# The attention's rows go to DRAM through GpSimd's DMA queue instead of SyncE's

## The chip, the cores and the metric

One Trainium2 chip (trn2), one of its cores. The time is device microseconds (us) of one execution of the program; the profile is one further execution of the same program, taken by the hardware profiler. The engines are named as the profile names them: PE (TensorE, matrix products), PEld (its weight loads), DVE (VectorE), ACT (ScalarE), POOL (GpSimd) and SP (SyncE, which computes nothing and starts DMAs). POOLq and SPq are the instruction queues of the last two, where their DMA starts stand.

## The reference

Block-causal attention for 8 batches of 8 heads, 576 tokens of 64 numbers, and then a mixture of 8 experts over the 4608 tokens of 512 numbers, of which each token takes the best one:

```python
scores = q @ k.T / sqrt(64)                  # per batch and head, 576 x 576
scores = where(row // 64 >= col // 64, scores, -1e9)
attn = exp(scores - max); attn /= attn.sum(-1) + 1e-09
x = (attn @ v)  ->  4608 rows (batch, token) of 512 (head, d)
logits = x @ w_gate                          # 8 experts
e = argmax(logits); g = softmax(logits)[e]; eom = sigmoid(x @ w_output_gate)
out[row] = g * eom[e] * (relu(x @ w1[e]) @ w2[e])
```

## The kernel before

**Stages.** The attention runs until about 420 us, the experts from there to the end at 825 us; the two overlap a little, since the first expert's work begins between the last pairs of heads. Rows of the attention's result pass from the one to the other through a DRAM buffer, `x_d` (4608 x 512 f32), from which the experts gather their tokens by index. A table in DRAM, `tab_d`, holds for each expert which rows are its own.

**One batch.** A batch is two units of four heads (16 units, u0 to u15), a unit is two pairs of heads (32 pairs). For each unit the function `Load` fetches k and q (`nat`, L91, 576 KB each), splits each into a high half (the cast of L96, on DVE) and a low half (the subtraction of L97, on POOL), transposes both by DMA (`tr`, L102) and copies two halves crosswise (`sw`, L107 and L108). For each pair, `load_v` loads the values of v (`va` L317, `vb` L319, `v8` L322), `softmax` makes scores on PE (`ps_s`, L335 to L338), their row maxima on DVE (`nmx`, L372, L393, L404) and from these the bias (`nbs`, L343, L406) of the exponentials on ACT (L355); `flip` transposes the probabilities on PE (L423) and copies them out (`pT`, L429); `values` multiplies by v (L438, L452) into `xT` (L453, L454).

**The end of a batch** is `finish_batch`. For each of five row tiles (64 rows, and four times 128) `rows(t)` transposes on PE (L469), normalizes on DVE into `xn` (L472) and writes `xn` to `x_d` (L476). `xn` has two buffers, so the third tile's L472 can only run when the first tile's write has landed, the fourth when the second's has, and so on. Between these rows stands the choice of the expert on DVE (L498 to L563), ending in the slots `sli` (L556) and the weights `idg` (L570), one small product on POOL (`z`, L565), and five scatters on POOL into `tab_d` (L574). After the last batch POOL reads the table (`ids`, L738) and gathers rows (`xg`, L749), which are cut and transposed (`xr`, `xt`) for PE (L889).

**What sets the order.** PE's order is written out by hand: generators (`softmax` of the next pair, `flip` and `values` of the present one, `finish_batch` of the batch before, `load_heads` two units ahead) are stepped in turns. The order of the other engines, and of the DMA starts on SP and POOL, is set when the program is built, by a scheduler that estimates when each instruction could start; each engine then executes its list strictly in that order. Each start of a DMA is an instruction on the engine that starts it; it waits there for its data and its buffer, and all behind it wait too.

```python
            x.split(0, nc.vector.tensor_copy, nc.gpsimd)     # L96 cast on DVE, L97 subtraction on POOL
        tr = sb.tile([P, MAXR, P], F16, name=f"tr{1 - i}")
        nc.sync.dma_start_transpose(tr, ...)                 # L102, on SP
        va = sb.tile([P, 4, D], F32, name="va", bufs=3)
        nc.sync.dma_start(va, v[b, hA, 0:512]...)            # L317, on SP
```

Of the kernel before, what the change touches and what calls it, by code (L numbers as in the profile page):

```python
# [26 lines left out]
def block_attention_top1_moe(  # L27
# [11 lines left out]
    nc = tc.nc  # L39
    B, H, S, D = q.shape  # L40
# [4 lines left out]
    Q0 = [0, 64, 192, 320, 448]  # L45
# [31 lines left out]
    x_d = dram.tile([NTOK, DM], F32, name="x_d")  # L77
# [380 lines left out]
    def finish_batch(b, sums, xT):  # L458
# [5 lines left out]
        def rows(t):  # L464

            r = ROWS[t]
            pm = ps_t.tile([P, 512], F32, name="ps_t")
            for g in range(NP):
                nc.tensor.transpose(pm[0:r, P * g:P * g + P], xT[:, g, Q0[t]:Q0[t] + r], ident)  # L469
            xn = sb.tile([P, DM], F32, name="xn")  # L470
            with tc.high_priority(offset=5):
                nc.vector.tensor_tensor(  # L472
                    xn[0:r].rearrange("p (h d) -> p h d", d=D), pm[0:r].rearrange("p (h d) -> p h d", d=D),
                    rec[0:r, t].unsqueeze(2).broadcast_to([r, H, D]), ALU.mult,
                )
            nc.sync.dma_start(x_d[b * S + Q0[t]:b * S + Q0[t] + r, :], xn[0:r])  # L476

        yield

# [1 line left out]
        for c0, c1 in ((0, 448), (448, 576)):  # L481
# [7 lines left out]
            yield  # L489
        yield  # L490
        rows(0)
        yield
        lh = small.tile([P, NT, H, 16], F32, name="lh", bufs=1)
# [38 lines left out]
        for t in range(1, NT):  # L532
            rows(t)
            yield
# [36 lines left out]
        for t in range(NT):  # L571
            r = ROWS[t]
# [379 lines left out]
    for p in range(B * NP):  # L952
        b, hp = divmod(p, NP)
# [161 lines left out]
```

## Time and profile before

| | |
|---|---|
| time, median of 3 runs | 823.86 us (822.45 to 830.36) |
| profiled execution, its own time | 826.82 us |
| its span from first to last instruction | 825.1 us |
| granted TensorE clock, mean | 0.982 |
| busy: PE, DVE, ACT, POOL | 764.0, 547.1, 517.5, 252.6 us |
| moved by hardware queues (SP) | 127.76 MB |
| moved by the software queue (POOL) | 19.29 MB |

The profiled execution's time is its span and 1.7 us around it, and lies 2.96 us above the median. Busy times say how much of the span an engine had an instruction in hand. An engine's idle time is put down to the event that came last before it went on ("releaser").

### The profile page before, as it was taken

The page shows a single profiled execution, that of the slowest core. Times are in us where ns is not written, and L with a number is a line of the kernel's source. Part 1 is how long each engine was busy: PE and PEld are TensorE (multiplying, and loading weights), DVE is VectorE, ACT ScalarE, POOL GpSimd, SP SyncE. Part 2 cuts the span into 40 slices and gives each one's busy share as a digit, 9 for nine tenths or more (in the row PEclk, how much of TensorE's full clock was granted, in tenths as well). Part 3 has the DMA queues.
Part 4 walks back from the last instruction along what each step waited for, and adds up shares of the span by engine and source line. Part 5 has one row for each costly group of instructions (what it writes and reads, how often), then busy time and mean ns, then how long its engine had stood idle before and what let it go on. Part 6 is the DMA issues. An engine that isn't in the chain of part 4 may idle for free. (4 is left out here: it accounts for less than half of the span.)

```text
span 825.1 us, 17693 instructions
## 1 busy us (share of the span) xinstructions
PE 764.0 (93%) x6466; PEld 512.7 (62%) x6466; DVE 547.1 (66%) x1200; ACT 517.5 (63%) x1207; POOL 252.6 (31%) x219
## 2 busy tenths in 40 slices
PE   4899988898989889778999999999999999999994
PEld 3566656565656656555686666676657666676652
DVE  5787858677676767858572866786566656786530
ACT  5788776777758667567513855765556555775530
POOL 4322312424122242447245432233212333200001
PEclk9999999999999999889999999999999999999998
DMA  8998997989898797996029899793789958721601
GB/s 153 168 185 174 192 176 148 176 150 184 173 205 151 155 183 157 191 226 177 28 83 270 152 369 257 220 275 99 249 264 280 274 188 281 179 50 48 230 27 41
DMA packets 255887, 148.25 MB, mean 180 GB/s; under 512 B 224561, under 2 KB 224625, under 8 KB 255793
## 3 DMA queue, kind: packets, MB, share of 16 engines
q1 hardware_dynamic: 247520, 127.76, 69.4%
q0 software_dynamic: 8272, 19.29, 7.6%
q8 instruction: 53, 0.87, 0.5%
q14 instruction: 42, 0.34, 0.1%
HBM read 122.23 MB, written 19.73 MB: 172 GB/s over the span
## 5 line engine op out<-in xcount | busy, mean ns | idle before, releaser
L889 PEld LDWEIGHTS <-w1b 128*128 128x128 f16 (+1 forms) x2112 | 182.6, 98 | 25.2 <-ACT ys L919 2.0
L355 ACT ACTIVATE pt<-ps_s,nbs 128x448 f32<-128x448 f32 (+1 forms) x314 | 164.4, 535 | 41.8 <-DVE nbs L343 17.9
L889 PE MATMUL ps_s<-xt,w1b 128*128 128x256 f16 (+3 forms) x1824 | 182.1, 261 | 1.8 <-DMA xt<-xr 1.5
L916 PE MATMUL ps_t<-w2b,hh 128*128 128x512 f16 x608 | 181.0, 379 | 0.0
L778 DVE TENSOR_TENSOR w2b<-w2f,w2b 128x1024 bf16<-128x1024 f32 x76 | 88.0, 1219 | 113.4 <-ACT w2b L777 113.4
L423 PE MATMUL ps_t<-ident,pt 128*128 128x128 f32 x800 | 124.5, 283 | 8.2 <-DVE xn L472 3.9
L429 ACT COPY pT<-ps_t 128x512 f32<-128x512 f32 (+3 forms) x222 | 96.5, 463 | 56.4 <-PE ps_t L423 55.6
L97 POOL TENSOR_TENSOR sp<-nat,sp 128x1152 f16<-128x1152 f32 x30 | 71.2, 2374 | 152.8 <-DVE nbs L343 91.7
L916 PE MATMUL ps_t<-w2b,hl 128*128 128x512 f16 x304 | 115.2, 379 | 0.0
L919 ACT ACTIVATE ys<-ps_t,ids 128x512 f32<-128x512 f32 x38 | 26.1, 687 | 136.1 <-PE ps_t L916 112.1
L335 PE MATMUL ps_s<-tr,tr 128*128 128x448 f16 (+1 forms) x378 | 98.8, 284 | 11.4 <-ACT pt L355 10.9
L920 POOL DMA_INDIRECT out_dram<-ys,ids x38 | 44.9, 1181 | 185.0 <-ACT ys L919 130.2
L916 PEld LDWEIGHTS <-hh 128*128 128x128 f16 x608 | 59.3, 98 | 66.8 <-issue 0.2
L423 PEld LDWEIGHTS ps_t<-ident,pt 128*128 128x128 f32 x800 | 87.3, 143 | 15.6 <-DVE xn L472 4.2
L336 PE MATMUL ps_s<-sw,tr 128*128 128x448 f16 (+1 forms) x378 | 91.4, 283 | 1.8 <-DMA sw<-tr 1.3
L438 PE MATMUL ps_a<-pT,va 128*64 128x512 f32 (+3 forms) x256 | 85.5, 457 | 6.8 <-DMA va<-in_v_dram 5.7
L778 DVE TENSOR_TENSOR w1b<-w1f,w1b 128x1024 bf16<-128x1024 f32 x76 | 88.1, 1218 | 0.5 <-ACT w1b L777 0.2
L393 DVE TENSOR_REDUCE nmx<-ps_s 128x2 f32<-128x896 f32 (+1 forms) x63 | 60.2, 955 | 41.7 <-PE ps_s L338 41.1
L438 PE MATMUL ps_a<-pT,vb 128*64 128x512 f32 (+3 forms) x256 | 85.6, 458 | 2.0 <-DMA vb<-in_v_dram 2.0
L777 ACT CAST w1b<-w1f 128x1024 f16<-128x1024 f32 x76 | 74.1, 1045 | 1.2 <-DMA w1f<-in_moe_w_dram 1.2
L777 ACT CAST w2b<-w2f 128x1024 f16<-128x1024 f32 x76 | 73.6, 1042 | 0.0
L355 ACT ACTIVATION_READ_ACCUMULATOR pt<-ps_s,nbs 128x1 f32 x314 | 65.2, 208 | 0.0
(203 smaller groups left out, 1080.2 us busy)
## 6 DMA issues: line engine op xcount, KB each, us to landing
w1f<-in_moe_w_dram SPq DMA_DIRECT2D x76, 512.0 KB
w2f<-in_moe_w_dram SPq DMA_DIRECT2D x76, 512.0 KB
nat<-in_k_dram SPq DMA_DIRECT2D x15, 576.0 KB
nat<-in_q_dram SPq DMA_DIRECT2D x15, 576.0 KB
sw<-tr SPq DMA_DIRECT2D x30, 288.0 KB
x_d<-xn SPq DMA_DIRECT2D x32, 256.0 KB
va<-in_v_dram SPq DMA_DIRECT2D x32, 128.0 KB
vb<-in_v_dram SPq DMA_DIRECT2D x64, 64.0 KB
```

Source lines behind the costliest of these rows:

```text
L97: last_lo[0] = lo.tensor_tensor(sp[:, :, 1, :], self.nats[i], sp[:, :, 0, :], ALU.subtract)
L335: nc.tensor.matmul(ps_ap, qq, k1[ab][:, c0:c1], start=True, stop=False)
L336: nc.tensor.matmul(ps_ap, qq, k2[ab][:, c0:c1], start=False, stop=last)
L355: last_exp[0] = nc.scalar.activation(to, ap, AF.Exp, bias=nbs[0:r, t, ab:ab + 1], scale=SCALE, accum_out=sums[0:r, t, hA + ab:hA + ab + 1],)
L393: nc.vector.tensor_reduce(nmx[:, t, :], pX[:, :, 0:n], AX.X, ALU.max, negate=True)
L423: nc.tensor.transpose(ps[:, i], probs[t][:, col:col + P], ident)
L429: copies[next(nth)](pT[:, r:r + m, Q0[t]:Q0[t] + rows], ps[:, i:i + m, 0:rows])
L438: nc.tensor.matmul(pa[64 * a:64 * a + 64, P * j:512], (va, vb)[a][:, j, :], pT[:, 1 + 2 * j + a, 64 + P * j:576], start=(j == 0), stop=False,)
L777: nc.scalar.copy(hi, src)
L778: eng.tensor_tensor(lo, src, hi, ALU.subtract)
L889: nc.tensor.matmul(ph[:, f4].rearrange("p (h n) -> p h n", n=P), wv[:, cc, f, :], xv[:, cc], start=(k == 0), stop=(k == 3 * KD - 1))
L916: nc.tensor.matmul(py, hv[:, f, h], wv[:, f, :], start=(k == 0), stop=(k == 3 * KF - 1))
```

## The change

All 40 writes of `xn` to `x_d` (8 batches of one write of 128 KB and four of 256 KB) are started by GpSimd instead of SyncE, and so go through the software queue. Nothing else is written differently:

```diff
                     rec[0:r, t].unsqueeze(2).broadcast_to([r, H, D]), ALU.mult,
                 )
-            nc.sync.dma_start(x_d[b * S + Q0[t]:b * S + Q0[t] + r, :], xn[0:r])
+            nc.gpsimd.dma_start(x_d[b * S + Q0[t]:b * S + Q0[t] + r, :], xn[0:r])
```

Since the order of all engines but PE is made anew at each build, the one line moves instructions elsewhere too. The writes leave SP's list and come into POOL's; PE's list is almost as it was; DVE's, ACT's and SP's lists are shuffled from the second batch's rows on.

On SP, the place around the sixth batch's writes and u15's transposes, before (`v_4959` is a pair's `v8`, the two numbered `tr` are those of u15):

```order
190 L476 DMA x_d<-xn 128x512
191 L317 DMA va<-in_v_dram 128x4x64
192 L319 DMA vb<-in_v_dram 64x4x64 x2
193 L322 DMA v_4959<-in_v_dram 128x1x64
194 L476 DMA x_d<-xn 128x512
195 L102 DMA_TRANSPOSE tr_5010<-sp 128x18x128
196 L476 DMA x_d<-xn 128x512
197 L102 DMA_TRANSPOSE tr_5039<-sp 128x18x128
198 L476 DMA x_d<-xn 128x512
199 L107 DMA sw<-tr_5010 64x2304
200 L108 DMA sw<-tr_5010 64x2304
201 L317 DMA va<-in_v_dram 128x4x64
```

And the same place now:

```order
170 L317 DMA va<-in_v_dram 128x4x64
171 L319 DMA vb<-in_v_dram 64x4x64 x2
172 L322 DMA v_4959<-in_v_dram 128x1x64
173 L317 DMA va<-in_v_dram 128x4x64
174 L319 DMA vb<-in_v_dram 64x4x64 x2
175 L322 DMA v_5170<-in_v_dram 128x1x64
176 L102 DMA_TRANSPOSE tr_5010<-sp 128x18x128
177 L102 DMA_TRANSPOSE tr_5039<-sp 128x18x128
178 L107 DMA sw<-tr_5010 64x2304
179 L108 DMA sw<-tr_5010 64x2304
```

The writes are gone, and the `va`, `vb` and `v8` of the pair that stood behind the transposes and the copies now stand ahead of them. The same happens at the transposes of two units before: of u11 (`va` and one `vb` move ahead) and of u13 (`va` and both `vb`).

On POOL, one batch (the first) between two groups of splits. Before:

```order
29 L97 TENSOR_TENSOR sp<-nat,sp 128x18x64 x4
30 L494 MEMSET lh 64x128
31 L565 TENSOR_TENSOR z<-L,oh 128x40
32 L574 DMA tab_d<-idg,sli 37120x2 x5
33 L97 TENSOR_TENSOR sp<-nat,sp 128x18x64 x4
```

And now:

```order
29 L97 TENSOR_TENSOR sp<-nat,sp 128x18x64 x4
30 L476 DMA x_d<-xn 64x512
31 L476 DMA x_d<-xn 128x512
32 L494 MEMSET lh 64x128
33 L476 DMA x_d<-xn 128x512
34 L565 TENSOR_TENSOR z<-L,oh 128x40
35 L476 DMA x_d<-xn 128x512 x2
36 L574 DMA tab_d<-idg,sli 37120x2 x5
37 L97 TENSOR_TENSOR sp<-nat,sp 128x18x64 x4
```

All five writes of a batch stand ahead of the five scatters, and so ahead of the split behind these. In the last batch one write stands between the second and the third scatter. In the sixth batch one of the splits of u15 stands between the first two writes.

On DVE, the cast of u10's k (`sp<-nat`), at the pair of heads that it goes with at about 215 us, before:

```order
380 L393 TENSOR_REDUCE nmx<-ps_s 128x2
381 L343 TENSOR_SCALAR nbs<-nmx 128x1 x2
382 L393 TENSOR_REDUCE nmx<-ps_s 128x2
383 L96 CAST sp<-nat 128x18x64
384 L343 TENSOR_SCALAR nbs<-nmx 128x1 x2
```

And now:

```order
377 L372 TENSOR_REDUCE nmx<-ps_s 128x2
378 L96 CAST sp<-nat 128x18x64
379 L343 TENSOR_SCALAR nbs<-nmx 128x1 x2
380 L372 TENSOR_REDUCE nmx<-ps_s 128x2
381 L429 COPY pT<-ps_t 128x3x128
382 L343 TENSOR_SCALAR nbs<-nmx 128x1 x2
383 L393 TENSOR_REDUCE nmx<-ps_s 128x2
```

The cast was behind both L393 of its pair and is now between that pair's first maximum (L372) and the bias that is made from it. The casts of k of u8, u12 and u14 moved up in the same way: u8's stands right behind the `pT` copy that follows L372, u12's ahead of L372, right behind the second L406 of the pair before, and u14's behind the first L404 of the pair before.

On DVE, the fourth batch's rows. Before:

```order
408 L525 TENSOR_REDUCE er<-eq 128x5
409 L343 TENSOR_SCALAR nbs<-nmx 128x1 x2
410 L527 TENSOR_TENSOR oh<-er,erev 128x40
411 L559 TENSOR_TENSOR d<-L,mx 128x40
412 L530 MEMSET oh 64x4
413 L546 TENSOR_REDUCE add<-oh 128x8
414 L567 TENSOR_REDUCE zs<-z 128x5
415 L472 TENSOR_TENSOR xn<-ps_t,rec 128x512
416 L393 TENSOR_REDUCE nmx<-ps_s 128x2
```

And now:

```order
410 L525 TENSOR_REDUCE er<-eq 128x5
411 L472 TENSOR_TENSOR xn<-ps_t,rec 128x512
412 L527 TENSOR_TENSOR oh<-er,erev 128x40
413 L393 TENSOR_REDUCE nmx<-ps_s 128x2
414 L530 MEMSET oh 64x4
415 L472 TENSOR_TENSOR xn<-ps_t,rec 128x512
416 L343 TENSOR_SCALAR nbs<-nmx 128x1 x2
417 L393 TENSOR_REDUCE nmx<-ps_s 128x2
```

The third row tile's L472 (row 415 before) moved up to right behind L525, and the fourth's, which stood behind the first L404, is now at row 415, between a maximum and its bias.

## Rows read from the trace of the kernel before

**Rows 1.** The page's first part: busy us (share of the span) and instructions of each engine.

```profile
PE 764.0 (93%) x6466; PEld 512.7 (62%) x6466; DVE 547.1 (66%) x1200; ACT 517.5 (63%) x1207; POOL 252.6 (31%) x219
```

**Rows 2.** Two stretches of the span (us), the attention and the experts: busy time of PE, PEld, DVE, ACT, POOL with their instructions, PE's granted clock, the DMA share and GB/s.

```profile
20.00:420.00 400.00, 361.28 (x3400) 238.91 (x3400) 289.40 (x896) 280.81 (x911) 134.21 (x100) 0.97 0.87 168
480.00:825.00 345.00, 334.34 (x2458) 224.10 (x2456) 207.99 (x198) 194.91 (x231) 79.42 (x68) 0.99 0.67 193
```

**Rows 3.** PE's waits between 20 and 420 us: the line that waited <- what it waited for, us in total, times, longest.

```profile
PE ps_a L438 <- DMA va<-in_v_dram: 5.7, 2, 3.7
PE ps_t L423 <- DVE xn L472: 3.9, 2, 3.7
...
PE ps_t L423 <- DVE nbs L406: 3.0, 3, 2.4
PE ps_t L452 <- DVE xn L472: 2.5, 2, 1.7
```

**Rows 4.** Four-us stretches of that view, behind PE's longer waits (the column behind POOL's busy time is PE's granted clock).

```profile
240.00:244.00 4.00, 3.10 (x23) 2.68 (x23) 2.97 (x11) 2.53 (x6) 1.03 (x2) 0.73 0.99 229
244.00:248.00 4.00, 4.00 (x26) 2.06 (x24) 2.94 (x13) 2.63 (x12) 3.08 (x4) 0.84 1.17 218
...
304.00:308.00 4.00, 4.00 (x17) 1.47 (x16) 0.67 (x1) 0.20 (x1) 0.00 (x0) 0.66 1.18 234
...
340.00:344.00 4.00, 3.33 (x28) 2.42 (x26) 2.15 (x7) 1.37 (x3) 2.08 (x3) 0.50 0.63 169
...
360.00:364.00 4.00, 4.00 (x15) 1.69 (x12) 1.00 (x3) 0.13 (x1) 0.00 (x0) 0.50 0.99 361
```

**Rows 5.** SP's list of DMA starts at u15's transposes: start us, duration, engine, line, operation.

```profile
342.23 2.86 SPq L102 DMA_TRANSPOSE tr<-sp  x1
...
352.26 0.81 SPq L317 DMA_DIRECT2D va<-in_v_dram  x1
```

**Rows 6.** SP's waits over the span, of the transposes (L102) for the split: us in total, times, longest.

```profile
SPq L102 <- POOL sp L97: 58.1, 19, 6.7
```

**Rows 7.** DVE at the fourth batch's rows: start us, duration, engine, line, operation, [idle before <- releaser].

```profile
229.20 0.68 DVE L472 TENSOR_TENSOR xn<-ps_t,rec 128x512 f32<-128x512 f32 x1
...
232.05 0.19 DVE L527 TENSOR_TENSOR oh<-er,erev 128x40 f16<-128x40 f32 x1
...
240.15 0.69 DVE L472 TENSOR_TENSOR xn<-ps_t,rec 128x512 f32<-128x512 f32 x1 [2.50 <-DMA x_d<-xn]
240.76 0.14 DVE L406 TENSOR_SCALAR nbs<-nmx 128x1 f32<-128x1 f32 x1
```

**Rows 8.** SP, the load of one k (first) and of k for u8, u10, u12, u14, each taken from its own stretch of SP's list.

```profile
48.07 0.47 SPq L91 DMA_DIRECT2D nat<-in_k_dram  x1
...
166.16 0.47 SPq L91 DMA_DIRECT2D nat<-in_k_dram  x1
...
214.41 0.46 SPq L91 DMA_DIRECT2D nat<-in_k_dram  x1
...
260.07 0.88 SPq L317 DMA_DIRECT2D va<-in_v_dram  x1
260.99 2.05 SPq L319 DMA_DIRECT2D vb<-in_v_dram  x2
...
263.68 0.47 SPq L91 DMA_DIRECT2D nat<-in_k_dram  x1
...
311.40 0.47 SPq L91 DMA_DIRECT2D nat<-in_k_dram  x1
```

**Rows 9.** DVE, the cast of the load at 48.07, and then the instruction behind which each of the four casts now stands (u8, u10, u12, u14).

```profile
53.60 0.76 DVE L96 CAST sp<-nat 128x1152 f16<-128x1152 f32 x1 [0.29 <-DMA nat<-in_k_dram]
...
169.06 0.56 DVE L429 COPY pT<-ps_t 128x384 f32<-128x384 f32 x1
...
215.60 0.75 DVE L372 TENSOR_REDUCE nmx<-ps_s 128x2 f32<-128x384 f32 x2 [0.38 <-PE ps_s L338]
...
262.28 0.15 DVE L406 TENSOR_SCALAR nbs<-nmx 128x1 f32<-128x1 f32 x1
...
311.89 0.76 DVE L404 TENSOR_REDUCE nmx<-ps_s 128x1 f32<-128x576 f32 x1 [0.86 <-PE ps_s L338]
```

**Rows 10.** POOL between z and the odd unit's split, third batch.

```profile
185.39 0.26 POOL L565 TENSOR_TENSOR z<-L,oh 128x40 f32<-128x40 f32 x1 [2.27 <-DVE oh L530]
193.33 0.94 POOL L574 DMA_INDIRECT tab_d<-idg,sli  x1 [7.69 <-DVE sli L556]
...
198.41 1.34 POOL L574 DMA_INDIRECT tab_d<-idg,sli  x1 [0.30 <-issue]
199.77 2.39 POOL L97 TENSOR_TENSOR sp<-nat,sp 128x1152 f16<-128x1152 f32 x1
```

**Rows 11.** The write's own line, x40: duration ns min/median/max of its start.

```profile
L476 SPq DMA_DIRECT2D x_d<-xn x40: 319/526/3009, 85.3 to 418.3; - x40
```

**Rows 12.** The scatters' own line: time from the start to the landing.

```profile
DMA to landing us min/median/max: 3.6/7.1/10.4
```

**Rows 13.** The start of the table's first write from POOL's queue (290 KB), and its landing.

```profile
L280 POOL DMA_DIRECT2D tab_d<-tinit x1: 742/742/742, 39.0 to 39.0; - x1
...
DMA to landing us min/median/max: 3.6/3.6/3.6
```

**Rows 14.** PE at the end of the attention: the wait for the first gathered tokens.

```profile
458.65 1.58 PE L889 MATMUL ps_s<-xt,w1b 128*128 128x256 f16 x13 [1.54 <-DMA xt<-xr]
```

## The prediction

> **What bounds the kernel now.** I read the engines' busy times first: PE 764 of 825 us, the others at two thirds or less [rows 1]. Then the stretches: in the experts' part PE has hardly a gap, in the attention's 361.3 of 400 us are busy [rows 2], so 38.7 us of idle PE are all that a change of the attention can win outright, and its clock stands at 0.97 on average there. Then PE's waits: 5.7 us for `va`, 3.9 and 2.5 us for `xn`, and 3.0 us for a bias [rows 3], the longest of which (2.4) is an `xn` too: at 240 us DVE stood 2.50 us in front of an L472 whose buffer was still being written out, and the bias queued behind it [rows 7]. Such a wait of DVE reaches PE nearly one to one. Last, the slices behind the long gaps: PE had stood still and then worked at a granted clock of 0.50 (1.2 of 2.4 GHz) in 340 to 344 and 360 to 364 us, and below 0.9 in three others [rows 4]. The work lost there is busy time times the missing clock: 1.7 us, 2.0, 1.4 (304 to 308), and 1.5 behind the gap at 240.
>
> So PE is the bound, broken by waits for DMAs and for DVE's order. The write itself is on nobody's path as work; what it does is to stand in a queue.
>
> **What the change removes.** SP loses 40 starts of 526 ns (median), 21.0 us [rows 11], none of which PE waits for by itself. What counts is what moves forward. At u15 the transposes were started from 342.23 on and the `va` that stood behind them only at 352.26 [rows 5]; PE waited 3.7 us for that `va`. Now this `va` stands ahead of the transposes, as it does at u13, where the other wait for `va` is. SP idles ahead of the transposes anyway, 19 times, 58.1 us in all, until POOL's split is done [rows 6], so I take both waits away: 5.7 us [rows 3] and the slow work behind them, 1.4 + 2.0 [rows 4]: **-9.1 us**. If the loads took the transposes' time instead, the transposes would start about one `va` and two `vb` later, 0.9 + 2.05 = 3.0 us [rows 8]; that is the other end for each of the two places, which I think unlikely.
>
> **What the writes cost on POOL.** A start of a plain write from POOL took 742 ns for 290 KB [rows 13], so 40 take 29.7 us, 3.7 a batch; the bounds are SP's 0.53 [rows 11] and the scatters' 0.94 to 1.34 [rows 10]. They stand ahead of the scatters, where POOL idled 2.27 and 7.69 us [rows 10]: these 10 us cover 3.7, and I cost them at 0. If the cover were gone, the split that follows the scatters without a gap (198.41 + 1.34, then 199.77) would start later by up to 3.7 us. After the last batch there is less cover: one write stands between two scatters, and PE waits 1.54 us for the first tokens [rows 14], so one start, **+0.7 us**, comes straight onto the end.
>
> The trace shows a scatter of 1.34 us beside others of 0.94 [rows 10], so POOL's starts can be held up by 0.4 us; at that price 40 writes would add 16 us to POOL, at most 2 a batch and still within the cover. By the Trainium skill, page "SBUF — State Buffer", section "SBUF: two separate sides", a DMA issued from GpSimd has its descriptors written by GpSimd, which DVE locks out during its two-port operations, and the page advises the ACT or SP queue: a rule against this change. Whether the 1.34 is that lock the trace doesn't say; by the rule the delay of each write is bounded by one DVE instruction beside it, and since those delays too would fall into the cover, the sum is the same by both.
>
> **The rows' own waits.** `xn(t)` waits for the landing of the write two before. By rows of the fourth batch: the second tile's `xn` is ready at 229.88, and through SP its write landed late enough that the fourth tile waited until 240.15 [rows 7]. Through POOL the write lands 3.6 us after its start at best [rows 13] and 7.1 as the scatters' median [rows 12], so at 233.5 to 237.0. But DVE gets to that L472 earlier now: it stands a few places behind the choice of the expert, which DVE reached at 232.05 [rows 7]; with the third tile's `xn` (0.69) and a maximum ahead of it, it comes at 232.9 to 233.9. It waits 0 to 4 us, around the 2.5 of before, and it again stands ahead of a bias. So I take this batch's wait as unchanged, 0, between a gain of all `xn` waits, 3.9 + 2.4 + 2.5 = 8.8 us with 1.5 + 1.7 of slow work behind them (-12.0), and a loss of one more such wait and its slow work, 2.4 + 1.5 = 3.9, in each of four batches (+15.6). In the sixth batch, where PE waited 3.7 us with 1.7 behind it, the rows and casts around are reordered altogether; there I take half, **-2.7 us**.
>
> **What moves against the kernel.** The casts of L96 have moved forward on DVE, and a cast that comes before its load holds DVE up. A load of k at 48.07 was waited for until 53.60 [rows 8, 9]: 5.5 us from start to use. The four casts, by the rows as they now stand:
> u8: loaded at 166.16 + 5.5 = 171.7, DVE there at 169.06 + 0.56 = 169.6: 2.1 us.
> u10: 214.41 + 5.5 = 219.9, DVE there behind the first of two L372 of 0.75 together, 216.0: 3.9 us.
> u12: 263.68 + 5.5 = 269.2; a `va` and a `vb` no longer stand between the copies and this load, 0.9 + 1.0 less, so 267.3; DVE there at 262.28 + 0.15 = 262.4: 4.9 us.
> u14: 311.40 + 5.5, less 3.0 for `va` and both `vb`, 313.9; DVE there at 311.89 + 0.76 = 312.7: 1.2 us.
> In sum 12.1 us of DVE. At one to one, as at 240 us, this is **+12.1 us** of PE. The ends are 0 (the loads come earlier, or PE has enough in hand) and, with a slow spell of 2.0 behind each of the two long waits, 16.1. I take the waits in full and no spell, since they may reach PE in pieces.
>
> **The sum.** -9.1 + 0.7 - 2.7 + 12.1 = +1.0 us. The profiled execution's 826.8 becomes 827.8; it stood 2.96 above the median of the runs, so on their scale 823.9 + 1.0, about **825 us**. A difference under 1%, some 8 us, is about what a measurement of this kernel can't tell from none.
>
> **Rivals.**
> *The loads are there when the casts come.* Then 12.1 us are not lost, and with half of the `xn` waits gone (6.0 in place of 2.7) the change is -9.1 + 0.7 - 6.0 = -14.4: 809.5 us; with all of them gone, 803.5. For it: SP is freed of 21 us of starts, and in the first batches two casts of k that waited did so for 0.3 us at the one shown, so the estimate of order and the landing are not far apart there. Against: nothing stood between the copies and the load of u10 that is now gone.
>
> *DVE's order loses more than is won.* The four casts draw their two slow spells (16.1), and two of the four batches get one more `xn` wait of 3.9 ahead of a bias: -9.1 + 0.7 + 16.1 + 7.8 = +15.5, 839.4 us. For it: three waits at just such places cost PE their full length and the clock behind them. It decides from the point at which the write lands later than 4 us after `xn`, or a load of k starts less than 5.5 us before DVE comes to its cast.
>
> *POOL becomes late.* If the last two writes of a batch come after `sli` instead of before, or their starts are slow, the scatters and the odd unit's split move by up to 3.7 us, in five batches 18.5, on top of the 1.0: 843 us. Against: 7.69 us idle ahead of the scatters.
>
> *It doesn't matter.* The bytes are the same, PE's order too, and what was waited for is only waited for elsewhere: 823.9. By the Trainium skill, page "DMA: Bandwidth & Descriptors", section "Issuing engines are not separate DMA queues", DMAs of any engine end on the same 16 DMA engines, and another issuer saves only the time of the start on the sequencer; by that alone the 21.0 us of SP would be the whole effect, which no engine waits for, and the time would stay. The trace has both queues share the DMA engines but shows no write of `x_d` through POOL's.
>
> **Chances.** The forecast 0.37 and no effect at all 0.05, together 0.42 within 1%; the loads in time 0.29, faster; DVE's order 0.22 and POOL 0.07, slower. The range must leave out a part of the fast case and a part of the slow ones: 808 to 841 us, which holds most of either case and the bounds of the terms in between.
>
> **What would show it.** Right: PE's waits for `va` at u13's and u15's transposes gone; DVE's L96 waiting for `nat` in four places by about 12 us together; L472 waiting for `x_d` about as long as before; POOL's idle time ahead of the scatters shorter by some 3.7 us a batch, the split still right behind them. Wrong: casts without waits (faster), a scatter that starts more than 1 us after `sli` (POOL late), transposes that start later against their split, or long idle PE with a low clock behind an L472.

## The result and the profile after

The changed kernel takes 833.12 us (median of 4 runs, 831.64 to 835.17) beside 823.85 for the kernel before: a ratio of 1.0125, 95% interval [1.0089, 1.0161]. In a later comparison it was 1.0091 [1.0064, 1.0118] (833.07 beside 825.77). Its profiled execution took 832.3 us against 826.8, so 5.5 us of the 9.3 between the medians are to be seen in the two traces; the rest lies in how the two profiled executions stood to their medians (3.0 above and 0.8 below).

The page of the changed kernel (busy times; queues):

```profile
PE 762.9 (92%) x6442; PEld 513.7 (62%) x6466; DVE 543.5 (65%) x1196; ACT 516.1 (62%) x1211; POOL 280.5 (34%) x259
...
q1 hardware_dynamic: 242272, 118.32, 60.4%
q0 software_dynamic: 11216, 28.73, 10.8%
```

The software queue moved 28.73 MB where it moved 19.29, POOL is busy for 28 us more than in [rows 1]: the writes did change their queue. The two stretches of [rows 2]:

```profile
20.00:420.00 400.00, 357.88 (x3363) 236.84 (x3362) 282.12 (x876) 279.16 (x913) 155.05 (x136) 0.96 0.79 166
480.00:825.00 345.00, 335.73 (x2461) 226.25 (x2478) 210.31 (x201) 196.41 (x233) 82.73 (x68) 0.99 0.64 194
```

PE's idle time in the attention is 42.1 us now, 38.7 before; the experts' stretch is as full as it was. What PE waited for between 20 and 420 us (line <- cause, us in total, times, longest), to be read beside [rows 3]:

```profile
PE ps_s L335 <- ACT pt L355: 24.2, 23, 6.6
PE ps_s L336 <- DMA sw<-tr: 7.7, 4, 2.3
...
PE ps_t L484 <- ACT lgT L488: 3.3, 1, 3.3
PE ps_t L423 <- DVE xn L472: 1.2, 2, 0.7
PE ps_t L469 <- DVE xn L472: 0.7, 1, 0.7
```

The waits for `va` (5.7 us) are gone altogether and those for `xn` nearly so (3.9 and 2.5, and 2.4 by way of a bias, before; 1.2 and 0.7 now). In their place stand 24.2 us of waits for exponentials (L355), which were 10.9, and 7.7 us for the copies `sw`, which were 1.3. DVE shows where the first of these come from (its waits for DMAs, same columns), and the four casts one by one, in the order u8, u10, u12, u14, the last with its neighbours:

```profile
DVE sp L96 <- DMA nat<-in_k_dram: 18.1, 6, 6.1
...
DVE xn L472 <- DMA x_d<-xn: 6.8, 6, 2.1
```

```profile
171.27 0.76 DVE L96 CAST sp<-nat 128x1152 f16<-128x1152 f32 x1 [1.08 <-DMA nat<-in_k_dram]
...
218.59 0.76 DVE L96 CAST sp<-nat 128x1152 f16<-128x1152 f32 x1 [3.88 <-DMA nat<-in_k_dram]
...
267.18 0.76 DVE L96 CAST sp<-nat 128x1152 f16<-128x1152 f32 x1 [5.52 <-DMA nat<-in_k_dram]
...
311.36 0.76 DVE L404 TENSOR_REDUCE nmx<-ps_s 128x1 f32<-128x576 f32 x1 [0.86 <-PE ps_s L338]
318.19 0.76 DVE L96 CAST sp<-nat 128x1152 f16<-128x1152 f32 x1 [6.08 <-DMA nat<-in_k_dram]
318.87 0.15 DVE L406 TENSOR_SCALAR nbs<-nmx 128x1 f32<-128x1 f32 x1
```

DVE stood 1.08, 3.88, 5.52 and 6.08 us in front of casts whose loads had not landed, 16.6 us together, with the bias of L406 or L343 behind them, and ACT's exponentials and PE's scores behind that. PE's gaps beside the last three are 1.7, 2.7 and 6.6 us. The casts of q that follow these moved up too, u10's from behind the pair's second L404 to ahead of its second L393, and waited for nothing.

### The profile page after: what moved, and what is told of

It is laid out like the page before. It is cut to its first block, busy times and chain, and to the rows that moved or that the text cites. A ratio compares the mean times of both kernels' runs of the same rounds, so it can differ in the third digit from the quotient of the medians.

```text
span 830.7 us, 17655 instructions
## 1 busy us (share of the span) xinstructions
PE 762.9 (92%) x6442; PEld 513.7 (62%) x6466; DVE 543.5 (65%) x1196; ACT 516.1 (62%) x1211; POOL 280.5 (34%) x259
## 3 DMA queue, kind: packets, MB, share of 16 engines
q0 software_dynamic: 11216, 28.73, 10.8%
## 5 line engine op out<-in xcount | busy, mean ns | idle before, releaser
L355 ACT ACTIVATE pt<-ps_s,nbs 128x448 f32<-128x448 f32 (+1 forms) x314 | 164.4, 534 | 49.3 <-DVE nmx L372 21.3
L916 PE MATMUL ps_t<-w2b,hh 128*128 128x512 f16 (+1 forms) x584 | 175.8, 379 | 0.0
L429 ACT COPY pT<-ps_t 128x512 f32<-128x512 f32 (+3 forms) x221 | 93.5, 454 | 46.5 <-PE ps_t L423 45.6
L335 PE MATMUL ps_s<-tr,tr 128*128 128x448 f16 (+1 forms) x378 | 99.0, 286 | 24.7 <-ACT pt L355 24.2
L336 PE MATMUL ps_s<-sw,tr 128*128 128x448 f16 (+1 forms) x378 | 91.6, 285 | 8.1 <-DMA sw<-tr 7.7
L438 PE MATMUL ps_a<-pT,vb 128*64 128x512 f32 (+3 forms) x256 | 87.5, 466 | 0.0
L438 PE MATMUL ps_a<-pT,va 128*64 128x512 f32 (+3 forms) x256 | 87.2, 465 | 0.0
L393 DVE TENSOR_REDUCE nmx<-ps_s 128x2 f32<-128x896 f32 (+1 forms) x63 | 60.1, 954 | 19.5 <-PE ps_s L338 19.0
L749 POOL DMA_INDIRECT xg<-x_d,ids x38 | 53.4, 1406 | 49.9 <-DMA ids<-tab_d 19.7
```

The source lines that it names most:

```text
L335: nc.tensor.matmul(ps_ap, qq, k1[ab][:, c0:c1], start=True, stop=False)
L336: nc.tensor.matmul(ps_ap, qq, k2[ab][:, c0:c1], start=False, stop=last)
L355: last_exp[0] = nc.scalar.activation(to, ap, AF.Exp, bias=nbs[0:r, t, ab:ab + 1], scale=SCALE, accum_out=sums[0:r, t, hA + ab:hA + ab + 1],)
L393: nc.vector.tensor_reduce(nmx[:, t, :], pX[:, :, 0:n], AX.X, ALU.max, negate=True)
L429: copies[next(nth)](pT[:, r:r + m, Q0[t]:Q0[t] + rows], ps[:, i:i + m, 0:rows])
L438: nc.tensor.matmul(pa[64 * a:64 * a + 64, P * j:512], (va, vb)[a][:, j, :], pT[:, 1 + 2 * j + a, 64 + P * j:576], start=(j == 0), stop=False,)
```

## The experiments

Each is compared with the kernel before on the same chip, and a ratio is the one to that. The chips differ: the kernel before takes 826.8 us on that of the first four versions, 839.2 on that of the next four, 825.8 on that of the last four. So ratios are compared, not times.

**Are the casts the loss?** Theory A: what the change loses, it loses by the place of four casts on DVE. Theory B: it is POOL or its queue. First the casts of k of u8, u10, u12 and u14 were put back, the writes staying on GpSimd:

```diff
-            hi(sp[:, :, 0, :], self.nats[i])
+            cast = hi(sp[:, :, 0, :], self.nats[i])
+            if i == 0 and self.u in (8, 10, 12, 14):
+                held.append(cast.ins)
...
+            while t == 3 and held:      # in softmax, behind the second L393
+                tc.add_manual_dep(held.pop(), mx3.ins.name, NOSYNC, reason="cast behind the maximum")
```

Expected: 

> The changed kernel, with the casts of k (L96) of u8, u10, u12 and u14 put back on DVE behind both L393 of their pair, as before the change; writes still on GpSimd. Theory A (DVE's order is the loss): the waits of these casts for their loads, 1.1 + 3.9 + 5.5 + 6.1 us in the trace after, vanish, and with them PE's gaps of 1.7, 2.7 and 6.6 us and about 5 us of slow work behind them, so some 10 to 16 us of 833: 817 to 824. Theory B (the writes make POOL or its queue late): the casts waited in the shadow of that, nothing is won: 830 to 835.

Measured: 823.29 us beside 826.79, ratio 0.9935 [0.9884, 0.9985]. And once more, on another chip, beside the changed kernel:

> The changed kernel with the four casts of k put back, again. Theory A: 1.5 to 2% below the changed kernel on a chip where the kernel before takes 824 to 827 us, ratio to the kernel before 0.989 to 0.996. Rival: no better than the changed kernel.

Measured: 824.16 beside 825.77, ratio 0.9988 [0.9957, 1.0019], where the changed kernel had 1.0091: 8.9 us or 1.1% less than that, and not the 1.5 to 2% that were expected. So about 1% of the time hangs on the place of four instructions of 0.76 us and on what the build moved with them (casts of the odd units stand elsewhere too), and with them put back the change is worth 0.1 to 0.65%. Of the trace of the second run (its profiled execution took 817.65 us, the lowest of its 12), PE's waits, and DVE's for k (lines are numbered 4 to 6 higher there, L339 is L335, L340 is L336, L478 is L472):

```profile
PE ps_s L339 <- ACT pt L359: 22.5, 29, 3.0
PE ps_s L340 <- DMA sw<-tr: 4.9, 3, 2.1
...
PE ps_t L429 <- DVE xn L478: 0.9, 2, 0.7
```

```profile
DVE sp L96 <- DMA nat<-in_k_dram: 7.2, 6, 2.7
```

DVE's waits for k went from 18.1 to 7.2 us (2.7 of them at a cast of an odd unit), but PE's waits for exponentials are still 22.5, in 29 pieces with none over 3.0, and the gap of 6.6 us is gone.

Then the counterpart: the kernel before, writes on SyncE, with the same four casts moved ahead. The build moved a little more with them: the casts of q that follow them went up too, from behind an L404 of their pair to ahead of its second L393, and a few starts on SP changed places:

```diff
+            cast = ahead_of.get(b * NP + hp)
+            with tc.issue_after(cast) if cast and t == 0 else nullcontext():
                 nc.vector.tensor_reduce(nmx[0:r, t, :], pX[0:r, :, sl], ...)
+            with tc.high_priority(offset=40), tc.issue_after(cast) if cast else nullcontext():
                 bias(t, r)
```

Expected: 

> The kernel before, writes on SyncE, with these four casts alone moved ahead, to between their pair's first L372 and its bias. Theory A: DVE waits there for the loads, by the rows of before 3.3 + 3.9 + 4.3 + 2.0 = 13.5 us, which reach PE nearly one to one, with slow work of 2 to 4 us behind them: 824 becomes 834 to 842. Theory B: the casts' place costs nothing by itself: 822 to 826.

Measured: 836.39 us, ratio 1.0091 [1.0048, 1.0134]. And again:

> The kernel before with these four casts alone moved ahead, again: ratio to the kernel before 1.005 to 1.014 by theory A, 0.998 to 1.002 by the rival that the casts' place costs nothing by itself.

Measured: 834.32, ratio 1.0120 [1.0075, 1.0164]. The four casts of this second run:

```profile
169.41 0.76 DVE L96 CAST sp<-nat 128x1152 f16<-128x1152 f32 x1 [1.85 <-DMA nat<-in_k_dram]
...
221.15 0.76 DVE L96 CAST sp<-nat 128x1152 f16<-128x1152 f32 x1 [3.51 <-DMA nat<-in_k_dram]
...
271.03 0.76 DVE L96 CAST sp<-nat 128x1152 f16<-128x1152 f32 x1 [3.07 <-DMA nat<-in_k_dram]
...
321.06 0.76 DVE L96 CAST sp<-nat 128x1152 f16<-128x1152 f32 x1 [3.24 <-DMA nat<-in_k_dram]
```

That is 11.7 us of waits on DVE (and 3.7 at the casts of q), and 8.6 us more than the kernel before beside it. Casts ahead of their loads give what the whole change gave, with no write on POOL. Theory A holds as far as that: their place is enough for a loss of this size. What B would add was tested next.

**Is POOL late?** Behind each write four memsets that nothing needs, meant to double its time on POOL (in the version with the casts put back):

```diff
+            with tc.issue_after(wr.ins):
+                for _ in range(4):
+                    nc.gpsimd.memset(idle, 0.0)
```

Expected: 

> The changed kernel with the four casts of k put back, and behind each write four memsets on GpSimd, some 0.8 us, that nothing needs: the time that a write takes on POOL is doubled, some 4 us more a batch. Theory A (POOL's idle time ahead of the scatters covers it): within 2 us of the version without them, ratio 0.99 to 0.996. Theory B (POOL is late): scatters, split, transposes come up to 4 us later in five batches, ratio 1.005 to 1.02.

Measured: 836.47 us, ratio 0.9915 [0.9866, 0.9963], on a chip where the kernel before took 839.23. POOL around the last write of the third batch (L483 is the write, L486 the memsets, L584 the scatter):

```profile
194.17 0.54 POOL L483 DMA_DIRECT2D x_d<-xn  x1 [1.28 <-DVE xn L479]
194.70 1.01 POOL L486 MEMSET idle<- 128x128 f32 x4
196.46 1.18 POOL L584 DMA_INDIRECT tab_d<-idg,sli  x1 [0.75 <-DVE idg L580]
```

The memsets took 1.01 us behind a write of 0.54. Even so POOL had still 0.75 us to wait for DVE's `idg` before the first scatter, and 0.6 to 1.1 in six of the first seven batches; in the fifth a split stood ahead of the last write, and the scatters followed the memsets without a wait for DVE. The ratio is below the 0.9948 that the changed kernel has on this chip, but the casts put back without the memsets were not run there, so it doesn't price the memsets. By the trace POOL isn't late, at nearly three times the price, in all of these batches but the fifth.

**Does the order of split and scatters matter?** The waits for `sw` point at a chain: `sli`, five scatters, split, transposes, `sw`. The odd unit's two splits were put ahead of the scatters, first in the changed kernel, then in the kernel before:

```diff
+            if i in (0, 1):                       # in split, behind the subtraction
+                for sc in behind.get(self.u, ()):
+                    tc.add_manual_dep(sc, last_lo[0].ins.name, NOS, reason="scatter behind the split")
...
+            if b < 5:                             # in finish_batch, behind a scatter
+                behind.setdefault(2 * b + 5, []).append(sc)
```

Expected: 

> The changed kernel, with both subtractions (L97) of the odd unit ahead of the five scatters on POOL instead of behind them, in the first five batches; DVE's order as in the changed kernel. Theory A with the chain scatters, split, transposes, sw, loads: transposes and the loads behind them come some 5 to 6 us earlier, PE's new waits for sw (7.7 us, with 4 us of slow work) vanish, and the casts of k find their loads or wait 0 to 1 us, so PE's gaps of 11 us and 5 us of slow work go too: 805 to 815. Theory B (the place of the casts in the order alone counts, or the writes on POOL): 828 to 835.

Measured: 826.91 us, ratio 0.9981 [0.9945, 1.0018]. The waits for `sw` fell to 0.8 us, and those of the casts to 1.9, 2.7, 1.1 and 4.2; PE waited 2.4 us for a `tr` and 3.2 us for a `va` instead, both in the first batch. So the chain was rightly seen, and of the 18 to 28 us that were hoped for 9 to 12 came (to 0.9981 from 1.0091 or 1.0125, which are ratios from other comparisons).

Expected: 

> The kernel before with the same move on POOL, writes on SyncE and DVE's casts where they were. Theory A: transposes come 5 to 6 us earlier, and with them va behind them (5.7 us of waits and 3.4 of slow work) and sw (1.3): 811 to 818. Theory B: 820 to 826, since before the change PE waited for the writes' rows and not for this chain.

Measured: 847.42 us, ratio 1.0232 [1.0196, 1.0268]: a clear miss, in the wrong direction. PE waited 12.9 us for `va`, 8.1 for `sw`, 5.5 for `tr`. Around the first batch's transposes, four-us stretches (busy time of PE, PEld, DVE, ACT, POOL; PE's clock; DMA share; GB/s), first of this kernel, then of the kernel before, from its own scatters on:

```profile
112.00:116.00 4.00, 3.99 (x51) 2.93 (x47) 1.70 (x6) 3.50 (x10) 0.78 (x1) 1.00 0.84 92
116.00:120.00 4.00, 1.32 (x14) 0.98 (x14) 1.27 (x5) 1.83 (x5) 0.00 (x0) 1.00 1.31 76
120.00:124.00 4.00, 0.35 (x1) 0.29 (x2) 0.85 (x6) 1.62 (x9) 0.00 (x0) 0.61 0.45 83
```

```profile
100.00:104.00 4.00, 4.00 (x50) 2.71 (x49) 3.11 (x7) 3.46 (x11) 3.67 (x3) 1.00 1.30 61
104.00:108.00 4.00, 1.58 (x20) 1.40 (x19) 2.70 (x6) 2.62 (x7) 2.79 (x2) 1.00 1.11 83
...
112.00:116.00 4.00, 4.00 (x43) 2.64 (x42) 2.37 (x7) 3.02 (x10) 0.00 (x0) 0.98 1.01 210
```

Behind the scatters (started from 106.6 to 111.8 us here) the DMA engines moved 76 to 92 GB/s, beside transposes, copies and loads that PE waits for. The kernel before moves as little behind its own scatters (started from 95.7 to 101.1), 61 and 83 GB/s from 100 to 108 us, and 193 to 216 only later, from 112 to 124 us. So the move didn't bring the low rate; it changed what meets it. What the scatters do to the other transfers wasn't measured by itself. The changed kernel with the same move has the same spell in its first batch (122, 72 and 80 GB/s from 112 to 124 us, with the waits for `tr`, `sw` and `va` named above), but not in the next four, where the kernel before waited again; why is open.

**Can both be had?** Two versions with the four casts put back: one with the odd units' casts put back too (k behind the second L393, q behind the second L404), one with the split ahead of the scatters in the second to fifth batch.

```diff
+            if self.u in ((8, 9, 10, 11, 12, 13, 14), (9, 11, 13))[i]:
+                held[i].append(cast.ins)
```

Expected: 

> The changed kernel, with the casts of k of u8 to u14 behind the second L393 of their pair and those of q of u9, u11 and u13 behind its second L404, as before the change; writes on GpSimd. Where only four casts of k were put back, the odd units' casts still waited 1.9 + 2.2 + 0.3 + 2.8 us for their loads, with gaps of PE of 2.2, 2.3 and 2.3. Theory A (a cast that stands ahead of its load costs PE its wait): these go, 6 to 9 us less than with four casts, a ratio to the kernel before of 0.983 to 0.987. Rival: the later casts make the odd split, its transposes and sw later, PE waits there instead (sw 6.4 us now, then 10 or more), ratio 0.99 to 1.00.

Measured: 844.00 us, ratio 1.0049 [1.0021, 1.0076]. The casts' waits went nearly (0.8 us for k, 0.5 for q), and still the time rose: PE waited 6.2 us for `sw`, and 5.6 for `xn`. The other, beside the four casts:

```diff
-            if b < 5:
+            if 1 <= b < 5:
                 behind.setdefault(2 * b + 5, []).append(sc)
```

Expected: 

> The changed kernel with the four casts of k put back and the odd unit's split ahead of the scatters in the second to fifth batch (not the first, where PE lost 6.4 us to transposes and va with that move). Theory A: the waits for sw (6.4 us with slow work behind them) go, ratio to the kernel before 0.975 to 0.985. Rival (the scatters' small writes, now beside the transposes and the sw copies, hold these up, as in the kernel before with the same move): ratio 0.995 to 1.02.

Measured: 844.18, ratio 1.0068 [1.0029, 1.0106]. PE had no wait for `sw` or `tr` left, and the time rose all the same. And the changed kernel as it is, with them:

> The changed kernel as it is, on the same chip as the others: a ratio of 1.009 to 1.016 to the kernel before, and in the trace the same waits of the casts of k of u10, u12 and u14 for their loads, 3 to 6 us each.

Measured: 837.20, ratio 0.9948 [0.9919, 0.9977]: the expected ratio was missed, though the casts of u10, u12 and u14 waited 2.4, 4.4 and 6.8 us. Both versions missed theory A's time, and neither rival's mechanism shows: `sw` cost no more in the first than with four casts put back (6.4 us), and nothing in the second. What took the gain back is open. All this is on the chip on which the kernel before took 839 us. There the changed kernel is not slower than the kernel before: that one lost 15 us on this chip, the changed one 4. No trace of the kernel before was taken on it, so where those 15 us lie is open. The four traces taken there have 4.2 to 6.4 us of PE's idle time between 20 and 430 us for which the profile names no releaser, and the other traces have none.

**Is the comparison itself sound?** The kernel before and the changed kernel, both without an edit, on the chip of the last four:

> The kernel before itself, once more, for its trace and its scatter beside the others: a ratio of 1 within 0.3%. If this chip gives it about 824 to 827 us, its trace has the waits for va and xn of the first profile; if it gives it 839 again, the trace shows where those 15 us lie (theory: DMAs that land later, so longer waits for va, vb and xn; rival: stalls of PE that no wait explains).

Measured: 825.90 beside 825.77, ratio 1.0008 [0.9976, 1.0041]; its trace has 6.2 us of waits for `va` and 3.9, 2.4 and 3.2 behind `xn`, as in [rows 3].

> The changed kernel, a third time. Theory A (it loses 16 us to casts ahead of their loads and wins some 10 elsewhere): ratio 1.008 to 1.016, where the kernel before takes 824 to 827 us; on a chip where that one takes 839, 0.993 to 1.000. Rival (the first comparison was chance): 0.995 to 1.003 on any chip.

Measured: 833.07, ratio 1.0091 [1.0064, 1.0118]; its casts waited 1.7, 3.7, 5.9 and 6.7 us. In the two comparisons in which the kernel before takes 824 to 826 us the loss is the same within its interval, with the same waits; chance as the rival is out there.

No version beats both kernels beyond doubt: the change with four casts put back was at 0.9935 and 0.9988, and the second interval holds 1.

## Why the prediction came out as it did

The forecast was 825 us, no change within 1%, in a range of 808 to 841. The time, 833, lies in the range, but the change was 1.25% and then 0.91%, a loss clear of the noise both times (and a gain of 0.5% on the chip on which the kernel before took 839 us). The time lies between the forecast and the rival "DVE's order loses more than is won" (839.4), which names the right mechanism, though the two further waits for `xn` in it didn't come. That the sum ended so near is in part luck: by the traces its gains and its losses were both about twice as large as forecast. Step by step:

**`va` (-9.1): right in size, wrong in one place.** Both waits went, and the slow spells behind them. At u15 it happened as told; SP's list there, now:

```profile
337.30 1.04 SPq L317 DMA_DIRECT2D va<-in_v_dram  x1
...
348.50 6.82 SPq L102 DMA_TRANSPOSE tr<-sp  x2
```

The `va` starts at 337.30, before the transposes, and not at 352.26 [rows 5]. This wait is in every trace that has the writes on SyncE and the scatters unmoved (3.6 to 4.7 us) and in none that has them on GpSimd. The other `va`, though, never stood behind u13's transposes. Before, it stood behind two writes:

```profile
291.19 2.90 SPq L476 DMA_DIRECT2D x_d<-xn  x2
294.19 0.41 SPq L317 DMA_DIRECT2D va<-in_v_dram  x1
...
299.82 3.66 SPq L102 DMA_TRANSPOSE tr<-sp  x1
```

It started at 294.19, after the writes (291.19) and ahead of the transposes (299.82), and PE waited for it to land at 303.7. It is not shown that its wait went because the writes left the queue: it is missing too in the second trace of the kernel before and in those of the kernel before with the casts ahead.

**Writes on POOL (0, and +0.7 at the end): right for the 0.** A start took 0.58 us and not 0.74, and the scatters still begin when DVE's `idg` is there, in the third batch at 193.41 as against 193.33 [rows 10]:

```profile
L476 POOL DMA_DIRECT2D x_d<-xn x40: 539/581/602, 83.6 to 424.6; - x40
...
DMA to landing us min/median/max: 2.3/2.9/5.9
```

```profile
191.12 0.54 POOL L476 DMA_DIRECT2D x_d<-xn  x1 [2.27 <-DVE xn L472]
193.41 1.18 POOL L574 DMA_INDIRECT tab_d<-idg,sli  x1 [1.75 <-DVE idg L570]
...
198.75 0.97 POOL L574 DMA_INDIRECT tab_d<-idg,sli  x1 [0.30 <-issue]
199.73 4.73 POOL L97 TENSOR_TENSOR sp<-nat,sp 128x1152 f16<-128x1152 f32 x2
```

The +0.7 is not to be seen: from the first to the last scatter of the last batch it is 5.9 us now and 5.6 before, and PE's wait of 1.54 us at 458 [rows 14], which it would have lengthened, is not there any more. The rule that DVE locks GpSimd out of writing descriptors (the Trainium skill, page "SBUF — State Buffer", section "SBUF: two separate sides") doesn't show in the starts, of which the 40 took 539 to 602 ns. Whether it is in some of the landings (2.3 to 5.9 us) the trace doesn't say.

**`xn` (-2.7): too little.** PE's waits of 8.8 us for `xn` [rows 3] fell to 1.9, with no slow spell behind them: some -10, where a bound was -12.0. The step that failed took the landings of other transfers of that queue for the writes' and so the wait of the fourth batch as unchanged: the writes landed after 2.9 us, not 3.6 to 7.1. But the landing isn't shown to be the reason. In the second trace of the changed kernel it took 4.1 us (median; 2.3 to 7.6), and PE's waits for `xn` were 1.7. In the kernel before with the casts ahead, writes on SyncE, they were 1.2 in the second trace. DVE itself still waited 6.8 us for landings, 10.1 before. A DVE that is held up elsewhere comes later to L472; how much of the -10 the queue won is open.

**Casts (+12.1): right mechanism, one term mis-sized.** Expected 2.1, 3.9, 4.9 and 1.2 us, measured 1.1, 3.9, 5.5 and 6.1. The last fails: the load of u14 was to come 3.0 us earlier, since a `va` and two `vb` no longer stand ahead of it. They don't, but the transposes do, and they began at 303.14 where they had begun at 299.82: that batch's `sli` came at 293.9 and not at 290.5, behind DVE's wait at u12.

```profile
303.14 5.68 SPq L102 DMA_TRANSPOSE tr<-sp  x2
...
311.08 1.40 SPq L91 DMA_DIRECT2D nat<-in_k_dram  x1
```

The load started at 311.08, as before (311.40), and was used at 318.19, 7.1 us later and not 5.5. I had held each cast's wait apart from the others; it feeds the next one.

**Slow spells: left out, and they came.** Stretches of four us behind the new waits, the clock in the third column from the end:

```profile
120.00:124.00 4.00, 4.00 (x22) 1.66 (x20) 1.86 (x5) 1.67 (x9) 0.03 (x1) 0.66 1.26 236
168.00:172.00 4.00, 4.00 (x22) 2.04 (x19) 2.30 (x9) 1.62 (x9) 0.00 (x0) 0.69 1.28 240
216.00:220.00 4.00, 3.54 (x20) 1.58 (x19) 1.41 (x5) 0.29 (x1) 0.56 (x1) 0.72 1.30 224
268.00:272.00 4.00, 1.75 (x7) 0.85 (x7) 3.12 (x11) 3.30 (x13) 3.29 (x2) 0.68 0.72 124
272.00:276.00 4.00, 4.00 (x25) 2.16 (x25) 1.31 (x3) 2.11 (x8) 1.44 (x1) 0.50 1.07 199
320.00:324.00 4.00, 4.00 (x19) 1.93 (x19) 2.13 (x8) 2.83 (x12) 3.01 (x2) 0.50 0.51 100
```

Missing clock times busy time gives 1.4, 1.2 and 1.0 us behind waits for `sw`, and 0.6 + 2.0 and 2.0 behind the casts of u12 and u14, where PE ran at 0.50 again, after gaps of 2.7 and 6.6 us. So of DVE's 16.6 us of waits 11.0 reached PE as gaps in this trace, not all as in the prediction, and with the slow work of 4.6 they come to 15.6, near the upper end of 16.1 that stood beside the 12.1. The runs price the casts lower: put back, they won 8.9 us beside the changed kernel on the same chip, and moved ahead in the kernel before they lost 9.6 and 8.6. Where these gaps close, others open.

Over the whole attention PE's idle time went from 38.7 to 42.1 us and the work lost to the clock (missing clock times busy time, summed over four-us stretches from 20 to 420 us) from 9.3 to 12.1, together 6.2 us, against 5.5 between the profiled executions. In the last comparison the clock is most of it. The kernel before, the changed kernel, and the changed kernel with the four casts put back (columns as in [rows 2]):

```profile
20.00:420.00 400.00, 361.95 (x3413) 241.11 (x3413) 291.11 (x904) 282.97 (x914) 135.72 (x101) 0.98 0.88 168
20.00:420.00 400.00, 360.67 (x3373) 237.54 (x3372) 283.07 (x878) 279.15 (x914) 155.30 (x137) 0.96 0.79 166
20.00:420.00 400.00, 360.29 (x3496) 241.51 (x3496) 298.06 (x929) 282.09 (x921) 164.56 (x145) 1.00 0.79 168
```

PE idled for 38.0, 39.3 and 39.7 us and lost 7.4, 13.3 and 0.0 us to the clock, in executions of 824.53, 831.66 and 817.65 us. The third is the lowest of its 12 (median 824.16), so not all of that is the casts'. But idle time alone doesn't tell the three apart.

**What wasn't foreseen: the wait for `sw`.** At four units (u5, u7, u9, u11) PE now waits for the copies, 7.7 us in all. At u9:

```profile
211.57 0.19 PE L335 MATMUL ps_s<-tr,tr 128*128 128x64 f16 x1
213.47 0.20 PE L336 MATMUL ps_s<-sw,tr 128*128 128x64 f16 x1 [1.71 <-DMA sw<-tr]
```

The chain behind a batch's `sli` begins no earlier: `sli` at 192.85 (192.88 before), scatters, split, transposes, and PE goes on with `sw` at 213.47. What PE gained by the vanished waits ahead of that point it can spend there. In the prediction a removed wait was money in hand, -11.1 us with the end's +0.7; with the four casts put back, the change won 3.5 and 1.6 us. I asked "what is late next" for the casts but not for the transposes, though one wait for `sw`, of 1.3 us, was in the trace of before. With the slow work behind them these waits come to some 11 us. They don't come from the writes on POOL alone: the kernel before with the casts ahead has 5.7 us of them too.

The sum by what was read in the two traces: -9.1 for `va`, -2.0 for `vb` (waits before, none now), -10 for `xn`, +15.6 for the casts, +10 for `sw` with its slow work (6.4 more than before, and 3.6); with 3.3 us of a new wait for `lgT` (L484) in the seventh batch, about +8 against 5.5 in the profile and 9.3 between the medians. The terms overlap and are not all of them, so the sum is rough, and the runs above bear out only the casts' share, at 9 us.

## What to carry to other kernels

Where a scheduler orders the engines, a change of queue is a change of order, and a single instruction that now stands ahead of its data can outweigh the transfer that was moved: compare the order on each in-order engine, and for each instruction that moved ahead of a load compare the time of that load's landing with the time at which the engine will come to it. Then pin the order of those few instructions and measure the change again; only that comes near to what the queue itself is worth, since the build moves more than what was pinned. Sum the clock's losses beside the idle time, too: here two executions with nearly the same idle time lay 7 us apart. And a wait that vanishes is won only up to the next chain that ends just behind it.

## What the runs showed of the hardware

The 40 writes (128 and 256 KB) from POOL's queue landed 2.9 us after their start in one trace of the changed kernel (the median; 2.3 to 5.9) and 4.1 us in another (2.3 to 7.6). The scatters, a few bytes per row through the same queue, took 4.0 and 4.8 us there, and 7.1 (3.6 to 10.4) in the kernel before [rows 12], whose other writes don't go through that queue. Behind the scatters, all DMA together moved 61 and 83 GB/s in the kernel before and 76 to 92 in the one with the split moved ahead, where 193 to 216 were moved a little later; what of that is the scatters' doing is open. That the split between the kernels depends on the comparison (ratio 1.0125 and 1.0091 in two, 0.9948 on the chip where everything is slower) I hadn't expected either, and it stays unexplained.
